# TensorE's first group in 64x64 tiles, other portions for the second group's convolution, and a new order for VectorE's copies of w_in

## The chip, the cores and the metric

The kernel runs on one core of one Trainium2 chip. The time is in device microseconds (us), the median of several runs; lower is better. A profile is one further execution, taken by the hardware profiler; its times count from the start of its span. Engines: PE is TensorE's matmul, PEld its weight load, DVE is VectorE, ACT ScalarE, POOL GpSimd, SP SyncE.

## What is computed

A light convolution over the sequence is followed by a two-layer network:

```python
w = softmax(weight, axis=-1)              # 8 heads x 7 taps
out = np.einsum('hk,bskhg->bshg', w, x_unf)   # x: 8 x 4096 x 192, zeros ahead of each sequence
x = out.reshape(B * S, D)
h = x @ w_in                              # 192 x 2048
g = np.maximum(0.01 * h, h)
return (g @ w_out).astype(np.float32)     # 2048 x 192
```

Every head has 24 of the 192 channels, and one set of 7 taps. Inputs and output are float32; inside, the kernel works in bfloat16 and accumulates in float32.

## The kernel before

**Layout.** The 8 sequences are treated as 4 pairs. A pair's data lies transposed in `xt`: channels in partitions, time along the row. The 192 channels are three chunks of 64 (`CH`); partitions 0 to 63 hold the chunk of the one sequence of the pair (`e` = 0), partitions 64 to 127 that of the other. `yt` holds the convolved data in the same layout. A block is 512 time steps of a pair; there are 32. The first two blocks are cut into halves of 256, called groups 0 to 3 (`groups`, L72); from group 4 on a group is a whole block.

**The stages of a group.** The convolution gives `yt`, by VectorE as seven multiply-adds for each chunk (`conv_jobs`, L209; L222 and L228), or, for parts of groups 0 and 1, by TensorE with diagonal matrices (`pe_conv_jobs`, L244; matmul at L259), whose sums are scaled out of PSUM (L271, L276). `mm1` (L488) multiplies `yt` by `w_in` into a PSUM tile `ph` of two banks (two such tiles are in turn use), and ScalarE's leaky ReLU (L515) makes `g` of it. A group of 256 takes eight steps `u`; each makes two column blocks of 128 hidden units for both sequences. The second layer then multiplies by `w_out`: for groups 0 to 3 in row form (`mm2_one`, L522; its matmul stands at L525), after that as L588 with VectorE's transposes (L610).

**Tiles of TensorE.** A matmul on 64 rows of weights and 64 columns uses a quarter of the array, and four of them may run abreast (64x64); 64x128 gives two abreast, and so does 128x64. In the profile the shape stands with the group, as `64*128`. `mm1` takes weight slices of M columns: M is 128 for groups 0 to 4 and 64 after that (L686). The convolution on TensorE is 64x64. The transposes of x (L167) are 128x64: 128 time steps by 64 channels.

**The first microseconds.** All is laid out by hand, and each engine runs its instructions in the order of the program (`manual_schedule`). Group 0's x is transposed first, then its convolution runs on TensorE (L459 to L474) until about 7.8 us. The loop at L670 then begins with group 0. It has no second-layer work yet. Between its steps of `mm1` the program puts, at fixed places: the transposes of group 1's x (`transpose_first(1)`, L502, inside u = 0), taken out of PSUM by VectorE (`evac_first`, L190, L195); the convolution of group 1, chunk 0 (`pe_0`) and chunk 2 (`pe_2`) on TensorE, in portions after the steps that `CUTS` (L53) names, and chunk 1 (`conv_1`) on VectorE; and after u = 6 the transposes of group 2's x. `pe_0` and `pe_2` have 14 jobs each of two matmuls; `pe_2` writes its halves crosswise (`cross`), so that its two scalings (`evac_2`) handle one half of the partitions each.

**w_in.** It comes in two halves `w_in[0]` and `w_in[1]` of 1024 columns, each by DMAs of rows 0 to 127 into slot 0 and rows 128 to 191 into slot 2. Since both partition halves need all three chunks, copies across the halves follow: `spread_down` (L322) copies slot 0's upper half to slot 1's lower, `spread_up` (L326) copies a lower half to an upper one: slot 0's to slot 1, slot 2's to slot 2. `near` and `far` are columns 0 to 511 and 512 to 1023 of a half. In group 0, steps u = 4 and 5 use the near columns of `w_in[1]`, and u = 6 and 7 the far ones.

**PSUM.** `ph` tiles take two times two banks. The pool `po` has four banks, given out in turn: for transposes, for the convolution's sums and for the second layer's sums. A new tile waits until the one four before it has been read.

**Later.** In group i from 1 on, VectorE convolves group i + 1 (L680). Group 4 is the first of 512. From group 2 on x arrives by DMA (group 2's by the transposes above), and the DMA's own transposes for group 3 (L199) and for blocks 2 and up (L114).

Of the kernel before, what the change touches and what calls it, by code (L numbers as in the profile page):

```python
# [11 lines left out]
BF16 = mybir.dt.bfloat16  # L12
# [3 lines left out]
def kernel(  # L16
# [8 lines left out]
    nc = tc.nc  # L25
# [10 lines left out]
    CH = 64  # L36
    NCH = D // CH
# [3 lines left out]
    HS = SUB // 2  # L41
# [8 lines left out]
    for k in range(K):  # L50
        SKEW += [(2, k), next(pair)]
    SKEW += [(1, 5), (0, 6), (1, 6)]
    CUTS = {1: (0, 6), 3: (6, 11), 5: (11, 14)}  # L53
    GB = 32
    NR = D // (2 * GB)

# [8 lines left out]
    psum_o = ctx.enter_context(tc.tile_pool(name="po", bufs=4, space=bass.MemoryType.PSUM))  # L65
# [56 lines left out]
    def new_xt(rp):  # L122
# [10 lines left out]
    x_rows = {  # L133
        q: const_pool.tile([128, 2, HS, D], BF16, name=f"x_rows{q}") for q in (1, 2)
    }
# [24 lines left out]
    ptr = {}  # L160

    def transpose_first(q, mid=None):
        if q:
            t = psum_o.tile([128, HS, NCH, 128], BF16, name="ptr", tag="po")
            for s, c in product(range(HS), range(NCH)):
                for e in range(2):
                    nc.tensor.transpose(  # L167
                        out=t[e * CH : (e + 1) * CH, s, c, :],
                        in_=x_rows[q][:, e, s, c * CH : (c + 1) * CH],
                        identity=ident,  # L170
                    )
            ptr[q] = [t[:, s] for s in range(HS)]
            return
        ts = [
            psum_o.tile([128, NCH, 128], FP32, name=f"ptr{s}", tag="po") for s in range(HS)
        ]
        for s, t in enumerate(ts):
            if s and mid is not None:
                mid()
            for c in range(NCH):  # L180
                nc.tensor.matmul(
                    out=t[:, c, :],
                    lhsT=x_half[q][:, c, s, :, :].rearrange("p e k -> p (e k)"),
                    rhs=ident,
                    start=True,
                    stop=True,
                )
        ptr[q] = ts

    def evac_first(q, *copies):  # L190
        dst = xt[0][:, :, HALO + q * HT : HALO + (q + 1) * HT]
        dst = dst.rearrange("p c (s k) -> p s c k", s=HS)
        for s, t in enumerate(ptr.pop(q)):
            for cs in (slice(0, 1), slice(1, NCH)) if q == 0 and s else (slice(0, NCH),):
                copies[s](out=dst[:, s, cs], in_=t[:, cs])  # L195

    def transpose_half(q):
# [82 lines left out]
    def run(*lists):  # L280
        for slots in zip_longest(*lists, fillvalue=()):
            for both in slots:
                for job in both:
                    job()
# [14 lines left out]
    for sign, off in ((1, 0), (-1, GRP - 1)):  # L299
        nc.gpsimd.affine_select(  # L300
            out=sel[:, :, 0, :], in_=sel[:, :, 0, :], compare_op=mybir.AluOpType.is_ge,
# [10 lines left out]
    near, far = slice(0, WF // 2), slice(WF // 2, WF)  # L312
# [8 lines left out]
    def spread_down(n, copy=nc.vector.tensor_copy, cols=slice(0, WF)):  # L321
        copy(out=w_in[n][0:CH, 1, cols], in_=w_in[n][CH:128, 0, cols])  # L322

    def spread_up(n, slots=slice(0, 3, 2), cols=slice(0, WF)):
        to = slice(slots.start // 2 + 1, (slots.stop - 1) // 2 + 2)
        nc.vector.tensor_copy(out=w_in[n][CH:128, to, cols], in_=w_in[n][0:CH, slots, cols])  # L326
# [10 lines left out]
    ident = const_pool.tile([128, 128], BF16)  # L337
# [10 lines left out]
    for h in range(2):  # L348
        cs = slice(h * NFC // (2 * RUN), (h + 1) * NFC // (2 * RUN))
        nc.gpsimd.dma_start(  # L350
            out=w_out.rearrange("p (c i) d -> p c i d", i=RUN)[:, cs],
            in_=moe_w_out.rearrange("(c p i) d -> p c i d", p=128, i=RUN)[:, cs],
# [5 lines left out]
    def warm(n, cols=HT, to=wa[:, 0]):  # L358
# [10 lines left out]
        out=nmax, in_=w9[:, 0:K], axis=mybir.AxisListType.X,  # L369
# [3 lines left out]
        out=w9[:, 0:K], in_=w9[:, 0:K], func=mybir.ActivationFunctionType.Exp,  # L373
# [18 lines left out]
    def select(out, parts):  # L392
# [17 lines left out]
        out=taps, in_=wps_hm[..., None].to_broadcast([128, NCH, 2, K + 1, 2])  # L410
# [5 lines left out]
    def diag_wide(c, p):  # L416
# [22 lines left out]
        out=rsum, in0=wml[:, :, K:], scalar=1e-9, in1=taps[:, :, 0, K:, 0],  # L439
# [14 lines left out]
    def act_scale(out, in_, scale):  # L454
# [11 lines left out]
        out=y_of(groups[0], 0), in0=hi[:, :HT], scalar=rsum[:, 0, :], in1=low,  # L466
# [21 lines left out]
    def mm1(grp, u, M):  # L488
        blk, t0, T = grp
        y = yt[blk]  # L490
        nf = ST // T
        ph = psum_h.tile([128, 2, ST], FP32, name="ph", tag="ph")
        chunks = range(NCH)


        wide = not (blk or t0 or u)
        order = [(i, c) for i in range(nf) for c in chunks]
        if wide:
            order = [(i, c) for c in chunks for i in range(nf)]
        for i, c in order:  # L500
            if wide and (i, c) == (0, 2):
                transpose_first(1)  # L502
            f = nf * u + i
            for e in range(2):
                ps = slice(e * CH, (e + 1) * CH)
                for m in range(0, 128, M):
                    nc.tensor.matmul(  # L507
                        out=ph[m : m + M, e, i * T : (i + 1) * T],
                        lhsT=w_in_of(f, e, c, m, m + M),
                        rhs=y[ps, c, t0 : t0 + T],  # L510
                        start=(c == chunks[0] and not (wide and i)),
                        stop=(c == chunks[-1]),
                        skip_group_check=wide,
                    )
        act = nc.scalar.activation(  # L515
            out=g[blk][:, nf * u : nf * (u + 1), :, t0 : t0 + T],
            in_=ph.rearrange("p e (i t) -> p i e t", i=nf),
            func=mybir.ActivationFunctionType.Prelu, alpha=0.01,
        )
        return act  # L520
# [149 lines left out]
    for i, grp in enumerate(groups):  # L670
        blk, t0, T = grp
        steps = T // 64
        if t0 == 0:
            g[blk] = g_pool.tile([128, NFC, 2, ST], BF16, name="g", tag="g")
        quota = plan.get(i, [16] * 4 if T == HT else [5, 5, 6, 5, 5, 6, 8, 8])

        if i == 0:
            ahead = []
        else:
            ahead = conv_jobs(groups[i + 1]) if i + 1 < len(groups) else []  # L680
        per = -(-len(ahead) // steps)
        for j in range(steps):
            early = between.get((i, j), (0, 0))
            for u in range(2 * j, 2 * j + 2):
                mm2_slots(i, early[u % 2])
                mm1(grp, u, 128 if i <= NSW else CH)  # L686
                if i == 0 and u == 0:
                    evac_first(1, nc.vector.tensor_copy, nc.vector.tensor_copy)
                    spread_up(0, slice(2, 3), far)
                    conv_1 = conv_jobs(groups[1], (1,))  # L690
                    run([conv_1[:3]])
                    spread_down(1)
                    spread_up(1, slice(0, 1), near)
                    spread_up(1, slice(2, 3))
                    run([conv_1[3:5]])
                    spread_up(1, slice(0, 1), far)
                    run([conv_1[5:]])
                    pe_0, evac_0 = pe_conv_jobs(groups[1], 0)
                    pe_2, evac_2 = pe_conv_jobs(groups[1], 2, cross=True)
                if i == 0 and u in CUTS:  # L700
                    cut = slice(*CUTS[u])
                    run(pe_0[cut], pe_2[cut])
                if i == 0 and u == 5:
                    evac_0(nc.vector.tensor_scalar_mul)
                    evac_2(nc.vector.tensor_scalar_mul, nc.vector.tensor_scalar_mul)
                if i == 0 and u == 6:
                    transpose_first(2)
                    evac_first(2, nc.vector.tensor_copy, nc.vector.tensor_copy)
            jobs = ahead[per * j : per * (j + 1)]
            if T == ST:  # L710


                jobs = ahead[len(ahead) * j // steps : len(ahead) * (j + 1) // steps]
                for job in jobs:
                    job()
                jobs = []
            mm2_slots(i, quota[j] - sum(early))
            if i == 1 and j == 1:
                load_x(3, transpose_x(2))
            for job in jobs:  # L720
                job()
            if i == 0 and j == 3:
                transpose_half(3)

            last_half = t0 + T == ST
            if i == NSW and j == steps - 1:
                evac_o(LAST - 1)
                slot = NSW * NR * NFC
            if j == steps // 4 and last_half and blk > 0:
                load_x(blk + 3)  # L730
            if j == steps // 2 and last_half and blk > 0:
                transpose_x(blk + 2)
# [35 lines left out]
```

## Time and profile before

| | |
|---|---|
| median of 3 runs | 680.72 us (680.7 to 681.06) |
| span of the profiled execution | 679.2 us |
| TensorE busy in it | 674.9 us, 99% |
| VectorE busy | 481.2 us, 71% |
| ScalarE busy | 517.6 us, 76% |
| granted TensorE clock | 1.000 |
| group 0's steps u begin, end about | 8.09, 17.1 us |
| first L507 of group 1, of group 4 | 17.37, 46.04 us |

The profiled execution is not one of the three timed runs; its time is known by its span, which counts from the first to the last instruction and is 1.5 us below the median. A timeline line gives start, length (both us), engine, line of the program, operation, output <- input, shape and count; `[0.20 <-issue]` says that the engine was idle for 0.20 us before it and what ended that. In it neighbouring instructions of one kind are merged. A line by stretch gives the stretch, its length, then busy time and number of instructions of each engine asked for, the granted clock, the DMA share and GB/s. The program's L numbers are those of the listing above.

### The profile page before, as it was taken

The page shows a single profiled execution, that of the slowest core. Times are in us where ns is not written, and L with a number is a line of the kernel's source. Part 1 is how long each engine was busy: PE and PEld are TensorE (multiplying, and loading weights), DVE is VectorE, ACT ScalarE, POOL GpSimd, SP SyncE. Part 2 cuts the span into 40 slices and gives each one's busy share as a digit, 9 for nine tenths or more (in the row PEclk, how much of TensorE's full clock was granted, in tenths as well). Part 3 has the DMA queues.
Part 4 walks back from the last instruction along what each step waited for, and adds up shares of the span by engine and source line. Part 5 has one row for each costly group of instructions (what it writes and reads, how often), then busy time and mean ns, then how long its engine had stood idle before and what let it go on. Part 6 is the DMA issues. An engine that isn't in the chain of part 4 may idle for free.

```text
span 679.2 us, 27092 instructions
## 1 busy us (share of the span) xinstructions
PE 674.9 (99%) x12442; PEld 446.3 (66%) x12442; DVE 481.2 (71%) x816; ACT 517.6 (76%) x601; POOL 147.4 (22%) x208
## 2 busy tenths in 40 slices
PE   9999999999999999999999999999999999999998
PEld 6997666666666666666666666666666666666667
DVE  7989477866768766778667687667786676876612
ACT  7899877777787777777777777778777777777781
POOL 8455221122211222211222112222022220000000
PEclk9999999999999999999999999999999999999999
DMA  9999755655737656556556566567365573321123
GB/s 149 99 119 104 52 85 83 84 64 67 96 74 93 76 54 86 84 85 86 66 63 92 80 92 78 56 83 94 73 87 69 60 96 71 72 56 33 34 49 94
DMA packets 213970, 53.27 MB, mean 78 GB/s; under 512 B 209312, under 2 KB 213536, under 8 KB 213856
## 3 DMA queue, kind: packets, MB, share of 16 engines
q0 software_dynamic: 98832, 13.97, 30.3%
q1 hardware_dynamic: 115008, 37.57, 28.0%
q8 instruction: 97, 1.59, 0.9%
q14 instruction: 17, 0.14, 0.1%
q10 hardware_dynamic: 16, 0.00, 0.0%
HBM read 28.31 MB, written 25.17 MB: 79 GB/s over the span
## 4 chain that ended last, share of the span: by engine, by line
PE 98%; DVE 1%; ACT 0%; issue 0%; ACTq 0%
PE ph L507 49%; PE acc L588 44%; PE po L525 5%; PE acc L259 0%; DVE diag L420 0%; PE ptr L167 0%; ACT L366 0%; ACTq L288 0%; DVE w_in L322 0%; DVE yt L465 0%; DVE o_sb L638 0%; DVE x_half L155 0%; ACT w L372 0%; DVE w_in L326 0%; ACT junk L366 0%
## 5 line engine op out<-in xcount | busy, mean ns | idle before, releaser
L515 ACT ACTIVATE g<-ph 128x1024 bf16<-128x1024 f32 x512 | 496.6, 1021 | 139.8 <-PE ph L507 139.6
L228 DVE SCALAR_TENSOR_TENSOR yt<-xt,wk,yt 128x512 bf16<-128x512 bf16 (+1 forms) x582 | 380.1, 715 | 0.2
L507 PE MATMUL ph<-yt,w_in 64*64 64x512 bf16 (+2 forms) x6048 | 377.5, 369 | 0.3 <-DVE yt L465 0.3
L588 PE MATMUL acc<-g,w_out 64*64 64x512 bf16 x5568 | 339.9, 376 | 0.0
L507 PEld LDWEIGHTS <-w_in 64*64 64x64 bf16 (+1 forms) x6048 | 229.7, 131 | 103.4 <-issue 1.1
L588 PEld LDWEIGHTS <-w_out 64*64 64x64 bf16 x5568 | 178.2, 118 | 118.8
L96 POOL DMA_DIRECT2D x_bf<-in_x_dram x180 | 133.9, 774 | 407.6 <-DMA xt<-x_bf 405.6
L610 DVE STREAM_TRANSPOSE o_t<-acc 128x512 f32<-128x512 f32 x87 | 72.9, 875 | 182.2 <-PE acc L588 182.2
L525 PE MATMUL po<-w_out,g 64*128 64x192 bf16 (+1 forms) x640 | 36.8, 243 | 0.0
L525 PEld LDWEIGHTS <-g 64*128 64x128 bf16 (+1 forms) x640 | 32.6, 95 | 3.2 <-issue 0.4
L222 DVE TENSOR_SCALAR yt<-xt,wk 128x512 bf16<-128x512 bf16 (+1 forms) x97 | 28.8, 320 | 2.4 <-DMA xt<-x_bf 2.4
L598 ACT COPY junk<-junk 128x1 f32<-128x1 f32 x58 | 11.1, 191 | 4.1
L638 DVE COPY o_sb<-po 128x192 f32<-128x192 f32 x8 | 2.8, 356 | 6.8 <-PE po L525 3.9
L638 ACT COPY o_sb<-po 128x192 f32<-128x192 f32 x16 | 5.1, 323 | 0.3
L259 PE MATMUL acc<-xt,diag 64*64 64x256 bf16 x126 | 4.7, 272 | 0.1
L149 POOL DMA_DIRECT2D x_half<-in_x_dram x6 | 4.3, 732 | 0.9 <-DMA w_in<-in_moe_w_in_dram 0.9
L259 PEld LDWEIGHTS <-diag 64*64 64x64 bf16 x140 | 3.7, 106 | 1.0 <-issue 0.4
L360 PE MATMUL warm<-const-bfloat16-1.0 128*128 128x512 bf16 (+2 forms) x8 | 3.3, 577 | 0.8 <-PEq L752 0.8
L145 POOL DMA_DIRECT2D x_rows<-in_x_dram x4 | 2.9, 746 | 0.0
L316 POOL DMA_DIRECT2D w_in<-in_moe_w_in_dram x5 | 2.9, 593 | 0.0
L360 PEld LDWEIGHTS <-const-bfloat16-1.0 128*128 128x128 bf16 x10 | 1.2, 128 | 2.2 <-issue 2.2
L326 DVE COPY w_in<-w_in 64x512 bf16<-64x512 bf16 (+1 forms) x7 | 2.3, 337 | 0.2
(52 smaller groups left out, 25.9 us busy)
## 6 DMA issues: line engine op xcount, KB each, us to landing
out_dram<-o_t SPq DMA_DIRECT2D x112, 192.0 KB, 4.7
x_bf<-in_x_dram POOLq DMA_DIRECT2D x180, 64.0 KB, 3.1
out_dram<-o_sb SPq DMA_DIRECT2D x8, 192.0 KB, 2.8
xt<-x_bf SPq DMA_TRANSPOSE x90, 3.2
w_out<-in_moe_w_out_dram POOLq DMA_DIRECT2D x2, 384.0 KB, 8.3
out_dram<-o_t SPq DMA_DIRECT2D x8, 96.0 KB, 2.4
out_dram<-o_sb SPq DMA_DIRECT2D x8, 96.0 KB, 1.7
w_in<-in_moe_w_in_dram POOLq DMA_DIRECT2D x2, 256.0 KB, 5.5
```

The source lines that it names most:

```text
L96: ins = nc.gpsimd.dma_start(out=t[:, c, :, e, :], in_=src[2 * rp + e, :, :, c * CH : (c + 1) * CH],)
L222: lambda s=src, d=dst, c=c: nc.vector.tensor_scalar_mul(d, s, wk[:, c, 0:1])
L228: lambda s=src, d=dst, c=c, k=k: nc.vector.scalar_tensor_tensor(out=d, in0=s, scalar=wk[:, c, k : k + 1], in1=d, op0=mybir.AluOpType.mult, ...
L259: lambda k=k, p=p, a=a, ps=ps, to=to, acc=accs[e]: nc.tensor.matmul(out=acc[to, :T], lhsT=diag[c][ps, p, k, :], rhs=xt[0][ps, c, a : a + T ...
L360: nc.tensor.matmul(out=to[:, 0:cols], lhsT=ones[:, 0:128], rhs=ones[:, 0:cols], start=True, stop=True,)
L507: nc.tensor.matmul(out=ph[m : m + M, e, i * T : (i + 1) * T], lhsT=w_in_of(f, e, c, m, m + M), rhs=y[ps, c, t0 : t0 + T], start=(c == chun ...
L515: act = nc.scalar.activation(out=g[blk][:, nf * u : nf * (u + 1), :, t0 : t0 + T], in_=ph.rearrange("p e (i t) -> p i e t", i=nf), func=my ...
L525: return nc.tensor.matmul(out=po[m], lhsT=g[b][ps, fc, e, s * 128 : (s + 1) * 128], rhs=w_out[ps, fc, :], start=start, stop=stop,)
L588: ins = nc.tensor.matmul(out=acc2[gi, r][e * CH : (e + 1) * CH, 0:T], lhsT=w_out_of(ps, fc, r), rhs=g[b][ps, fc, e, t0 : t0 + T], start=fi ...
L598: seal = nc.scalar.copy(out=junk, in_=junk)
L610: nc.vector.transpose(out=osb[gi, 0][:, 0 : T // GB, :, r], in_=acc2.pop((gi, r))[:, 0:T].rearrange("p (j k) -> p j k", k=GB),)
L638: ins = copy(out=o_sb[:, n % 2, :], in_=po.pop(n))
```

## The change

- `mm1` uses slices of 64 columns in group 0 as well (`128 if 0 < i <= NSW else CH`), so that each 64x128 matmul becomes two of 64x64, four abreast.
- The transposes of the x of groups 1 and 2 go in 64x64 tiles: each of 128 time steps by 64 channels becomes two of 64 by 64. The two halves of time (`r`) write to two PSUM tiles `ptr0` and `ptr1` in place of one; `evac_first` copies one tile each, in runs of 64 elements in place of 128.
- The convolution of group 1 on TensorE has its portions after u = 1, 2 and 3 (5, 5 and 4 jobs of each list) in place of u = 1, 3 and 5 (6, 5 and 3). Its sums are scaled after u = 3 in place of u = 5.
- On VectorE four of the seven steps of `conv_1` come before the copies of `w_in[1]`, in place of three. The copies are six of 512 columns, the near ones first, in place of four (two of 1024 columns). The other three steps of `conv_1` come between and behind the scalings.

```diff
-    CUTS = {1: (0, 6), 3: (6, 11), 5: (11, 14)}
+    CUTS = {1: (0, 5), 2: (5, 10), 3: (10, 14)}
...
         if q:
-            t = psum_o.tile([128, HS, NCH, 128], BF16, name="ptr", tag="po")
+            ts = [
+                psum_o.tile([128, HS, NCH, CH], BF16, name=f"ptr{r}", tag="po")
+                for r in range(2)
+            ]
             for s, c in product(range(HS), range(NCH)):
-                for e in range(2):
+                for r, e in product(range(2), range(2)):
+                    ps = slice(r * CH, (r + 1) * CH)
                     nc.tensor.transpose(
-                        out=t[e * CH : (e + 1) * CH, s, c, :],
-                        in_=x_rows[q][:, e, s, c * CH : (c + 1) * CH],
-                        identity=ident,
+                        out=ts[r][e * CH : (e + 1) * CH, s, c, :],
+                        in_=x_rows[q][ps, e, s, c * CH : (c + 1) * CH],
+                        identity=ident[ps, ps],
                     )
-            ptr[q] = [t[:, s] for s in range(HS)]
+            ptr[q] = ts
             return
...
+        if q:
+            dst = dst.rearrange("p c (s r k) -> p r s c k", s=HS, r=2)
+            for r, t in enumerate(ptr.pop(q)):
+                copies[r](out=dst[:, r], in_=t)
+            return
...
-                mm1(grp, u, 128 if i <= NSW else CH)
+                mm1(grp, u, 128 if 0 < i <= NSW else CH)
                 if i == 0 and u == 0:
                     evac_first(1, nc.vector.tensor_copy, nc.vector.tensor_copy)
                     spread_up(0, slice(2, 3), far)
                     conv_1 = conv_jobs(groups[1], (1,))
-                    run([conv_1[:3]])
-                    spread_down(1)
+                    run([conv_1[:4]])
                     spread_up(1, slice(0, 1), near)
-                    spread_up(1, slice(2, 3))
-                    run([conv_1[3:5]])
+                    spread_down(1, cols=near)
+                    spread_up(1, slice(2, 3), near)
+                    spread_down(1, cols=far)
                     spread_up(1, slice(0, 1), far)
-                    run([conv_1[5:]])
+                    spread_up(1, slice(2, 3), far)
...
-                if i == 0 and u == 5:
+                if i == 0 and u == 3:
                     evac_0(nc.vector.tensor_scalar_mul)
-                    evac_2(nc.vector.tensor_scalar_mul, nc.vector.tensor_scalar_mul)
+
+                    def after(n):
+                        def scale(*args):
+                            run([conv_1[n : n + 1]])
+                            nc.vector.tensor_scalar_mul(*args)
+
+                        return scale
+
+                    evac_2(after(4), after(5))
+                    run([conv_1[6:]])
```

## The prediction

> **What bounds the kernel now.** I read the page first, then busy time by stretch, then the timelines of the weight loads, VectorE and ScalarE over the changed microseconds, and last the hand-over at 46 us.
>
> ```profile
> PE 674.9 (99%) x12442; PEld 446.3 (66%) x12442; DVE 481.2 (71%) x816; ACT 517.6 (76%) x601; POOL 147.4 (22%) x208
> PE 98%; DVE 1%; ACT 0%; issue 0%; ACTq 0%
> ```
>
> TensorE is busy all the way and is nearly the whole chain of waits, so time can only be gained by starting its long steady part earlier. A busy PE may still be draining. The stretches (PE, PEld, DVE, ACT, POOL busy):
>
> ```profile
> 8.09:17.29 9.20, 9.20 (x181) 7.21 (x181) 8.09 (x21) 8.01 (x10) 7.03 (x12) 1.00 1.24 162
> 17.29:46.04 28.75, 28.75 (x608) 28.56 (x606) 28.71 (x65) 26.37 (x34) 17.30 (x23) 1.00 1.19 109
> ```
>
> The changed code runs in the first. In the second VectorE is as full as TensorE: it convolves groups 2, 3 and 4 without a pause, and that matters below. The weight loads (PEld) show what the mixed tiles cost:
>
> ```profile
> 10.11 0.58 PEld L259 LDWEIGHTS <-diag 64*64 64x64 bf16 x24 [0.20 <-DVE xt L195]
> 10.89 1.24 PEld L507 LDWEIGHTS <-w_in 64*128 64x128 bf16 x24 [0.20 <-issue]
> 12.33 0.47 PEld L259 LDWEIGHTS <-diag 64*64 64x64 bf16 x20 [0.20 <-issue]
> 13.00 0.25 PEld L507 LDWEIGHTS <-w_in 64*128 64x128 bf16 x5 [0.20 <-issue]
> 13.46 1.02 PEld L507 LDWEIGHTS <-w_in 64*128 64x128 bf16 x19 [0.21 <-DVE w_in L326]
> ```
>
> Each change of shape has 0.20 us of idle in front. In the convolution before 8 us, four 64x64 matmuls of 256 columns start every 0.109 us (6.28, 6.39, 6.50 ...), so the 24 from 10.11 should last 0.656; the next shape starts 0.78 later. A change therefore costs 0.125 net. The row at 13.46 is a real wait: the second half of w_in was not yet copied across the partition halves.
>
> **TensorE, part by part.** (a) Between 8.09 and 17.02 there are ten changes of shape (into and out of transposes twice, convolution three times). All go; one comes in before L525, which keeps 64x128. Nine times 0.125 is 1.13 us. (b) Group 0's 96 matmuls of 64x128 become 192 of 64x64. A pair of the old takes 0.109, a quad of the new 0.109 by the convolution rows: nothing gained or lost. (c) Each set of 12 transposes becomes 24. Pitch goes with columns in the trace: 0.216 for 512 (46.04 on), 0.109 for 256, 0.055 for the present 128. For 64 columns no row exists. Low end 0.028 a quad (0.17 a set), high end today's 0.055 (0.33, no gain, if the weight load sets the pace); I take 0.17, on the line of the three rows: 0.16 saved twice. (d) The convolution is 56 matmuls in either cut. So at most 1.13 + 0.32 = 1.45 us of TensorE work goes, and less survives, as the walk shows.
>
> A rule speaks against (c). The trace starts the four matmuls of a quad within 0.01 us of each other. The Trainium skill ("TensorE: Matmul & The Clock Gate", Back-to-back issue gap) gives 1 to 64 columns a floor of about 25 ns from start to start; no row here has so few columns. By it a set would take 24 x 25 = 600 ns, u7 below would end 0.35 later, and the forecast would be 680.5 in place of 680.4.
>
> **The walk.** A quad is 0.109, a step u of group 0 six quads, 0.656. The start, 8.09, stays: it follows VectorE's yt (L465). First two chunks to 8.53, transposes to 8.70, then a wait: yt's third chunk leaves VectorE at 8.39 + 0.49 = 8.88, so 8.93 (with 0.05 for the release, as at 46.21 below) to 9.15. u1 to 9.81. The convolution needs xt from VectorE (9.22 + 0.62 = 9.84, unchanged, as those copies stand behind a w_in copy that ends at 9.20): 9.89 to 10.44. u2 11.09, convolution 11.64, u3 12.30, convolution 12.73. u4 needs three w_in copies, which VectorE ends at about 12.50, 12.81 and 13.11 (below): its third quad starts at 13.17, u4 ends at 13.60, u5 at 14.26. From here ScalarE limits: an activation of g takes 1.02 and they follow at 0.92 to 1.02, longer than a bare u, with two ph buffers. By these rows it starts 0.31 after a step's last quad:
>
> ```profile
> 14.13 2.98 ACT L515 ACTIVATE g<-ph 128x1024 bf16<-128x1024 f32 x3 [0.41 <-PE ph L507]
> 17.33 2.99 ACT L515 ACTIVATE g<-ph 128x1024 bf16<-128x1024 f32 x3 [0.22 <-PE ph L507]
> ```
>
> u4's activation runs 13.80 to 14.82, u5's 14.72 to 15.74. So u6 runs 14.87 to 15.53, transposes to 15.70, u7 15.79 to 16.45. One change of shape and three pairs of L525 (0.25) bring group 1's first matmul to 16.83, where it is at 17.37 now. w_out's first half is no obstacle: POOL's wait for it ends at 16.02. The new bank order puts L525's second bank behind the last scaling of group 1's third chunk, about 16.50 on VectorE, before 16.58. TensorE alone would be 0.54 earlier.
>
> **VectorE.** Its rows now:
>
> ```profile
> 10.59 1.00 DVE L228 SCALAR_TENSOR_TENSOR yt<-xt,wk,yt 128x256 bf16<-128x256 bf16 x2
> 12.21 0.42 DVE L322 COPY w_in<-w_in 64x1024 bf16<-64x1024 bf16 x1 [0.61 <-DMA w_in<-in_moe_w_in_dram]
> 12.64 0.77 DVE L326 COPY w_in<-w_in 64x512 bf16<-64x512 bf16 x2
> 13.45 1.00 DVE L228 SCALAR_TENSOR_TENSOR yt<-xt,wk,yt 128x256 bf16<-128x256 bf16 x2
> 14.48 0.29 DVE L326 COPY w_in<-w_in 64x512 bf16<-64x512 bf16 x1
> 14.80 1.00 DVE L228 SCALAR_TENSOR_TENSOR yt<-xt,wk,yt 128x256 bf16<-128x256 bf16 x2
> 15.72 0.48 DVE L271 TENSOR_SCALAR yt<-acc,rsum 128x256 bf16<-128x256 f32 x1
> 16.23 1.00 DVE L276 TENSOR_SCALAR yt<-acc,rsum 64x256 bf16<-64x256 f32 x2
> 17.27 0.62 DVE L195 COPY xt<-ptr 128x384 bf16<-128x384 bf16 x2
> ```
>
> From 12.21 to 17.27 are 5.06 us: copies 1.56, four conv steps 1.95, three scalings 1.55. One conv step (0.52) moves into the 0.61 of idle before 12.21, where the w_in DMA hides it; 0.06 of idle is left. Four copies become six of 512 columns. At the 0.29 of the rows at 8.07, 8.91 and 14.48, plus gaps of 0.01 to 0.03, they make 1.80. The upper end is 0.55, what a downward copy of 512 took at 6.97: six at that are 3.4. I take 0.29, since in this same stretch the downward copy took 0.42 for twice the columns. The sum is 1.80 + 1.46 + 1.55 = 4.81, **0.25 earlier**. The regrouped copies of the transposes stay at 0.31 each, same elements; their shorter runs could make them 0.05 dearer, which is nothing beside the ends above.
>
> Group 1's second chunk now ends VectorE's list, at 17.0, 0.1 later than TensorE wants it; the lead there shrinks to 0.44. What then decides stands 29 us later:
>
> ```profile
> 17.26:46.16 28.90, 28.86 (x65) 1.00 1.19 109
> 45.42 0.73 DVE L228 SCALAR_TENSOR_TENSOR yt<-xt,wk,yt 128x512 bf16<-128x512 bf16 x1
> 46.21 0.11 PEld L507 LDWEIGHTS <-w_in 64*128 64x128 bf16 x1
> ```
>
> The first row is VectorE alone, 28.86 busy of 28.90: all it does up to 46.16 hangs on when it began, at 17.27. Its last conv step of group 4 ends at 46.15, and at 46.21 a weight load follows that TensorE needs for 46.26. The slack there is 0.05. So a lead on TensorE is cut to VectorE's 0.25 plus 0.05: **0.30 us** remain, and nothing later waits that nearly: VectorE idles again from 46.16.
>
> **Sum.** The profiled span is 679.2; the median of the runs shown is 680.72, about 1.5 above, which I take as what lies around the span and as unchanged. 679.2 - 0.30 = 678.9, and so **680.4**.
>
> **Rivals.** (1) TensorE's whole lead arrives, because VectorE's copies overlap (as 12.64 and 12.85 do, by 0.08) and its list ends 0.45 earlier: 680.1 to 680.2. For it: several conv steps and scalings would also overlap. Against it: today's rows have mostly gaps. (2) Slower: w_in's last part comes late, at VectorE's third copy. It is issued at 6.13 and lands 6.6 later, 12.73; the copy wants it at 12.81. TensorE's instructions are loaded by DMA too (page, queue q8): one load between 9 and 11 us, the next between 16 and 18, each some 0.96 us of one engine (3.0% of 16 engines over 2 us). With 1.6 times the instructions the second load comes near 12 us. If it stands before w_in's last rows, VectorE's third copy starts 0.9 late: -0.30 becomes +0.6, 681.3. It turns slower than before from a delay of 0.3 us on. The same case holds copies at 0.55: the two downward ones add 0.5 (680.9), all six 1.6 (682.0). Against it: the load may use another engine. (3) A load of instructions stalls TensorE itself in 8 to 16 us, where it now eats 8 instructions per 0.109 us, twice the steady rate. No PE row shows such a wait today; the convolution before 8 us ran at that rate for 84 matmuls. One or two loads of 0.96, less the 0.24 by which TensorE's lead exceeds what arrives: 681.2 to 682.1. (4) The change doesn't do what it says: four small tiles with w_in's strided weights don't run abreast. At half speed that is 5.2 us more, 685. Against it: L507 runs 24 such matmuls of 512 columns in 1.30 us throughout the steady part.
>
> **How the numbers follow.** Forecast 0.55; (1) 0.17; (2) 0.19; (3) 0.06; (4) 0.01; a gain past (1), by an order of things later on that I don't see, 0.02. The range takes the forecast, (1) and (2) with its bounds: 679.8 to 681.9. About 0.2%, 1.36 us, is what a measurement of this kernel can tell from no change. The likeliest cases lie within it: over 0.2% faster, 0.03 (more than all that (a) and (c) remove); over 0.2% slower, 0.06 ((4), the far ends of (2) and (3)); within, 0.91.
>
> **What would show it.** Right: no 0.20 idle between 8.7 and 16 us, one before L525; group 0 in quads 0.109 apart; VectorE without idle before 12.15; its copies of the transposes near 17.0; group 1's matmuls near 16.9; the end of VectorE's convolution near 45.9 with TensorE's wait just after it. Wrong: w_in copies of 0.5, an idle before the third, PE rows waiting on issue inside a shape, or a shift on TensorE at 46 us that is not VectorE's.

## The result, and the profile after

The changed kernel takes 683.82 us (median of 5 runs, 683.38 to 685.21) against 681.06 for the kernel before in the same runs: 1.0045 times as long, 95% interval 1.0034 to 1.0056. The forecast was 680.4, the range 679.8 to 681.9; the changed kernel is slower by 2.8 us and lies outside. The profiled execution spans 681.9 us, 2.7 more than before.

Most lines shift by nine: `mm1`'s matmul is now L516, the convolution L268, the second layer's row form L534; the transposes move from L167 to L171. The page's chain of waits and the groups of costliest instructions that answer to the first lines shown of before:

```profile
PE 674.6 (99%) x12562; PEld 447.9 (66%) x12562; DVE 482.1 (71%) x818; ACT 517.7 (76%) x601; POOL 147.7 (22%) x208
...
PE 98%; DVE 1%; issue 1%; ACT 0%; ACTq 0%
...
L516 PE MATMUL ph<-yt,w_in 64*64 64x512 bf16 (+3 forms) x6144 | 379.0, 368 | 2.4 <-issue 1.8
...
L268 PE MATMUL acc<-xt,diag 64*64 64x256 bf16 x126 | 4.7, 271 | 1.1 <-issue 1.0
```

The same two groups before, in which hardly any idle time stood:

```profile
L507 PE MATMUL ph<-yt,w_in 64*64 64x512 bf16 (+2 forms) x6048 | 377.5, 369 | 0.3 <-DVE yt L465 0.3
...
L259 PE MATMUL acc<-xt,diag 64*64 64x256 bf16 x126 | 4.7, 272 | 0.1
```

TensorE's busy time is 0.3 us less, yet the span grew. The new share in the chain is "issue": time in which TensorE waited for nothing that the profile shows, 1.8 us within `mm1` and 1.0 us within the convolution. The timeline of the weight loads shows where (idle time before a row in brackets):

```profile
8.09 0.41 PEld L516 LDWEIGHTS <-w_in 64*64 64x64 bf16 x15 [0.59 <-issue]
...
10.38 0.78 PEld L516 LDWEIGHTS <-w_in 64*64 64x64 bf16 x24
...
12.43 0.47 PEld L268 LDWEIGHTS <-diag 64*64 64x64 bf16 x19 [1.25 <-issue]
12.87 0.72 PEld L516 LDWEIGHTS <-w_in 64*64 64x64 bf16 x24
...
14.95 0.67 PEld L516 LDWEIGHTS <-w_in 64*64 64x64 bf16 x24 [0.20 <-issue]
16.05 0.56 PEld L516 LDWEIGHTS <-w_in 64*64 64x64 bf16 x20 [0.42 <-issue]
18.63 0.14 PEld L516 LDWEIGHTS <-w_in 64*64 64x64 bf16 x3 [2.02 <-issue]
```

The idle 0.20 at each change of shape is gone, as it should be. In its place stand two stops, and neither is at a place where the program waits: the first comes one weight load into a portion of the convolution, the second after 20 of the 24 matmuls of step u = 6. By stretches of TensorE (stretch, length, busy time and number of matmuls, granted clock, DMA share, GB/s):

```profile
8.09:11.41 3.32, 3.29 (x116) 1.00 1.03 146
11.41:12.43 1.02, 0.00 (x0) 1.00 1.35 169
12.43:16.82 4.39, 4.14 (x128) 1.00 1.32 188
16.82:18.63 1.81, 0.00 (x2) 1.00 1.31 85
```

Ahead of the first stop TensorE works as forecast, with 116 matmuls in 3.3 us. The stops take 1.02 + 1.81 = 2.83 us. Group 1's first matmul is at 20.08 (17.37 before, +2.71), group 4's at 48.75 (46.04, +2.71), the end at 681.9 (+2.7): what is lost before 19 us is never won back. Between the two stops lie 128 matmuls with 128 weight loads, 256 instructions.

### The profile page after: what moved, and what is told of

Read it like the earlier page. It is cut to its first block, busy times and chain, and to the rows that moved or that the text cites. A ratio compares the mean times of both kernels' runs of the same rounds, so it can differ in the third digit from the quotient of the medians.

```text
span 681.9 us, 27334 instructions
## 1 busy us (share of the span) xinstructions
PE 674.6 (99%) x12562; PEld 447.9 (66%) x12562; DVE 482.1 (71%) x818; ACT 517.7 (76%) x601; POOL 147.7 (22%) x208
## 4 chain that ended last, share of the span: by engine, by line
PE 98%; DVE 1%; issue 1%; ACT 0%; ACTq 0%
PE ph L516 49%; PE acc L597 44%; PE po L534 5%; DVE diag L429 0%; PE acc L268 0%; ACT g L524 0%; ACT L375 0%; ACTq L297 0%; DVE w_in L331 0%; DVE yt L474 0%; PE ptr L171 0%; DVE o_sb L647 0%; DVE x_half L155 0%; ACT w L381 0%; DVE w_in L335 0%
## 5 line engine op out<-in xcount | busy, mean ns | idle before, releaser
L516 PE MATMUL ph<-yt,w_in 64*64 64x512 bf16 (+3 forms) x6144 | 379.0, 368 | 2.4 <-issue 1.8
L516 PEld LDWEIGHTS <-w_in 64*64 64x64 bf16 (+1 forms) x6144 | 231.9, 131 | 104.9 <-issue 3.2
L534 PE MATMUL po<-w_out,g 64*128 64x192 bf16 (+1 forms) x640 | 37.8, 243 | 0.0
L534 PEld LDWEIGHTS <-g 64*128 64x128 bf16 (+1 forms) x640 | 34.0, 95 | 2.4 <-issue 0.4
L607 ACT COPY junk<-junk 128x1 f32<-128x1 f32 x58 | 11.1, 191 | 4.1
L268 PE MATMUL acc<-xt,diag 64*64 64x256 bf16 x126 | 4.7, 271 | 1.1 <-issue 1.0
L268 PEld LDWEIGHTS <-diag 64*64 64x64 bf16 x140 | 4.0, 106 | 1.8 <-issue 1.3
```

Source lines behind the costliest of these rows:

```text
L268: lambda k=k, p=p, a=a, ps=ps, to=to, acc=accs[e]: nc.tensor.matmul(out=acc[to, :T], lhsT=diag[c][ps, p, k, :], rhs=xt[0][ps, c, a : a + T ...
L516: nc.tensor.matmul(out=ph[m : m + M, e, i * T : (i + 1) * T], lhsT=w_in_of(f, e, c, m, m + M), rhs=y[ps, c, t0 : t0 + T], start=(c == chun ...
L534: return nc.tensor.matmul(out=po[m], lhsT=g[b][ps, fc, e, s * 128 : (s + 1) * 128], rhs=w_out[ps, fc, :], start=start, stop=stop,)
L607: seal = nc.scalar.copy(out=junk, in_=junk)
```

## The theory and its rival

**Theory A.** TensorE's instructions are loaded by DMA (queue q8) in blocks of 256. Two blocks fit; the next one is asked for when a block is used up, and TensorE stops when it reaches a block that is not there. In the first 20 us the load queues behind data. The change puts 240 more instructions before 20 us and so reaches the blocks' limits too early.

**Theory B.** The stops are waits among the engines that the new order makes: VectorE's copies and scalings, or the PSUM banks, which the transposes now take in pairs.

In the trace before, the q8 loads begin at 9.94, 16.50, 20.57, 26.71 and 32.96 us. From the third on, each begins 0.2 to 0.6 us after the moment when TensorE passes another 256 recorded instructions (702 at 20.38, 958 at 26.41, 1214 at 32.36). Counted back, the first two were asked for at about 7.1 and 13.8, and were 2.8 and 2.7 us late. The request is not in the trace; its time is this count.

## The experiments

**mm1 alone.** One edit to the kernel before:

```diff
-                mm1(grp, u, 128 if i <= NSW else CH)
+                mm1(grp, u, 128 if 0 < i <= NSW else CH)
```

> The kernel before with one part of the change: group 0's mm1 in 64x64 tiles, 192 more instructions on TensorE before 17 us. Theory A (instruction loading): TensorE's instructions come by DMA in blocks of 256; the load of a block starts only when the block two before it is used up, waits 3 to 5 us behind data in the first 20 us, and TensorE stops when it reaches a block that has not come. Then TensorE stops with 'issue' near 11.3 us until about 12.4 and again near 16.5 until about 18.6, and the median is 682.5 to 683.9. Theory B (a wait among the engines made by the new order: VectorE's copies and scalings, or the PSUM banks given to the transposes in pairs): no stop longer than 0.5 us here, 680.0 to 681.0.

Measured: 684.85 us against 681.08, ratio 1.0054 (1.0042 to 1.0067), above the range expected. The clock has a share in that: three of the six executions, the profiled one among them, have a mean granted clock of 0.998 and took 685.58 to 686.20 us; the other three, at 1.000, took 683.45 to 684.13. (What the clock did comes last below.) The stops are there, without the new order and without banks in pairs, and now in other places of the program, the second in the middle of the transposes:

```profile
13.24 0.41 PEld L507 LDWEIGHTS <-w_in 64*64 64x64 bf16 x15 [1.13 <-issue]
...
19.17 0.14 PEld L167 LDWEIGHTS <-x_rows 128*64 128x64 bf16 x3 [1.83 <-issue]
```

What the places have in common is the count. These are the stretches up to each stop's end, first of the changed kernel, then of this one (stretch, length, then busy time and count of PE, PEld, DVE, ACT, POOL):

```profile
0.00:12.42 12.42, 10.12 (x222) 7.04 (x223) 9.12 (x35) 8.96 (x17) 11.52 (x26) 1.00 0.90 136
12.42:18.62 6.20, 4.14 (x128) 3.56 (x128) 4.31 (x12) 3.02 (x4) 3.94 (x6) 1.00 1.32 158
```

```profile
0.00:13.23 13.23, 11.31 (x222) 7.94 (x223) 9.51 (x36) 9.07 (x17) 11.38 (x25) 1.00 0.87 133
13.23:19.16 5.93, 4.21 (x128) 3.60 (x128) 3.93 (x9) 3.98 (x4) 4.63 (x7) 1.00 1.36 155
```

In both, TensorE stops after 222 matmuls and 223 weight loads, and again after 128 more of each, whatever the instruction is. Theory B has no reason for that.

**The transposes alone**: `transpose_first` and `evac_first` of the change put into the kernel before.

```diff
-            t = psum_o.tile([128, HS, NCH, 128], BF16, name="ptr", tag="po")
+            ts = [
+                psum_o.tile([128, HS, NCH, CH], BF16, name=f"ptr{r}", tag="po")
+                for r in range(2)
+            ]
...
```

> The kernel before with only the transposes of groups 1 and 2 in 64x64 tiles (48 more instructions on TensorE, two PSUM banks a set). Theory A: the block limits are reached about 0.6 and 1.0 us earlier than before (13.1 and 19.3 us), still after the loads are there (12.4 and 18.6): no stop, 680.6 to 681.3. Theory B, if the banks in pairs are the cause: a stop of 0.5 us or more in 9 to 19 us, 681.5 or above.

Measured: 681.08 against 681.08, ratio 1.0001 (0.9992 to 1.0009), no stop. The banks in pairs are not the cause.

**The order alone**: the new `CUTS`, the portions and VectorE's new order, all tiles as before.

```diff
-    CUTS = {1: (0, 6), 3: (6, 11), 5: (11, 14)}
+    CUTS = {1: (0, 5), 2: (5, 10), 3: (10, 14)}
...
-                    run([conv_1[:3]])
-                    spread_down(1)
+                    run([conv_1[:4]])
...
```

> The kernel before with only the new portions of the convolution and the new order on VectorE (no instruction more on TensorE). Theory A: no stop; by the forecast's sum for VectorE 0 to 0.3 us earlier, 680.7 to 681.1 against 681.0. Theory B, if the order is the cause: TensorE stops for 1 us or more between 11 and 19 us, 682 or above.

Measured: 681.66 against 681.08, ratio 1.0008 (1.0000 to 1.0017), above the 680.7 to 681.1 expected. No stop of the kind, but no gain either: at the edge of what can be told, it is slower.

**All but mm1**: the change with `128 if i <= NSW else CH` put back.

> The change with group 0's mm1 left in 64x128 tiles (48 more instructions than before, in place of 240). Theory A: no stop over 0.5 us that ends with an instruction block, 680.6 to 681.7. If the transposes or the order together make the stops: 683 or above.

Measured: 681.50 against 680.75, ratio 1.0011 (1.0002 to 1.0020), no stop of the kind. So both stops hang on `mm1`'s 192 instructions; the 0.75 us that are lost without them are something else. The 48 instructions of the transposes already come to the edge: in this run and the one with the transposes alone the first block's load ended at 11.51 and 11.55 us, and the first instruction behind the limit began 1.38 and 1.39 us later, as soon after the load as at the end of the stops (1.3 to 1.46).

The profile of this run also shows why the order gains nothing, in the weight loads, in the only wait of `mm1`'s matmuls for ScalarE (us in total, times, longest) and in ScalarE's activation of u = 4:

```profile
15.38 0.59 PEld L516 LDWEIGHTS <-w_in 64*128 64x128 bf16 x11 [0.62 <-DVE yt L237]
```

```profile
PE ph L516 <- ACT g L524: 0.5, 1, 0.5
```

```profile
14.31 1.02 ACT L524 ACTIVATE g<-ph 128x1024 bf16<-128x1024 f32 x1 [0.32 <-PE ph L516]
```

Step u = 6 starts 0.05 us after that activation ends (14.31 + 1.02 = 15.33): it waits for the `ph` buffer, as the row of the matmuls says, and VectorE is named for the weight loads by a release that lies near. In the kernel before, a portion of the convolution stood after u = 5 and filled ScalarE's time; now they are all spent by u = 3. Group 1's first matmul comes at 17.41 here, 17.37 before. This execution was the fastest of the eleven (680.91), and its span, 679.2, is that of the kernel before: it shows that there is no gain, and not where the median loses 0.75, which stays open.

**Tiny matmuls**, the direct test of a count: the kernel before with 64 extra matmuls that compute nothing anyone reads.

```diff
+    for n in range(64):
+        r, e = divmod(n % 4, 2)
+        ps = slice(r * CH, (r + 1) * CH)
+        nc.tensor.matmul(
+            out=(wps, wa)[r][e * CH : (e + 1) * CH, 1, 500:504],
+            lhsT=ones[ps, 0:CH], rhs=ones[ps, 0:4], start=True, stop=True,
+        )
     spread_up(0, slice(0, 1), far)
```

> The kernel before with 64 extra matmuls of 4 columns in 64x64 tiles (128 more instructions), put where TensorE idles 0.4 us ahead of group 0; they write to unused columns of PSUM and nothing of the change is in it. They take some 0.5 us of TensorE, of which 0.4 is idle time. Theory A (blocks of 256 instructions come late): the block limit that was crossed at 13.7 us is now reached at about 10.5, the block is there at about 12.4, so TensorE stops for 1.5 to 2 us, and the median is 682.2 to 683.0. If only the new tiles or the new order make the stops: 680.9 to 681.4.

Measured: 683.15 against 680.75, ratio 1.0036 (1.0024 to 1.0049), but this decides nothing: `wps` was still being read by ScalarE, and the tiny matmuls waited 1.1 us for that. TensorE then came to the limit late and stopped there for less than 0.4 us. The repeat writes to `wa` alone (`out=wa[e * CH : (e + 1) * CH, r, 500:504]`):

> The run with 64 tiny matmuls again, their results now in a PSUM tile that no engine still reads, so that they don't wait for ScalarE as they did (1.1 us, which spoiled that run). The kernel before otherwise. Theory A: the block limit is reached at about 10.5 to 10.8 us, the block is usable 1.4 us after its load ends (11.0 to 11.2), so TensorE stops for 1.4 to 2 us within the convolution or the steps there, and the median is 682.0 to 682.8 (before: 680.8). Without such a limit the added matmuls cost at most 0.5 us: 680.8 to 681.4.

Measured: 683.66 against 681.23, ratio 1.0033 (1.0021 to 1.0045), more than expected. The stretch up to the stop's end, and the two stretches of TensorE that hold the stop and what follows:

```profile
0.00:13.85 13.85, 9.87 (x222) 6.88 (x222) 9.62 (x36) 8.08 (x16) 11.39 (x25) 1.00 0.87 135
```

```profile
11.00:13.90 2.90, 0.34 (x16) 1.00 1.21 178
13.90:17.30 3.40, 3.40 (x36) 0.50 1.47 188
```

The old tiles, the old order, the old banks, and TensorE stops at the same count (444 in the records, 445 in the others), for 2.83 us, in the convolution: its block's load began only at 11.48 us here. That settles A against B. The last row is a second price: the granted clock was 0.50 for 3.4 us after the stop. It was paid in this execution, the slowest of the six (685.47, mean clock 0.997); the other five, at 1.000, took 682.92 to 684.03.

**Do the loads wait behind data?** First only the data of later groups were put off, from 10 us to behind group 0's step 5 (`load_first(3)` and `load_x(2)` with a dependency on its activation), in the changed kernel:

```diff
-    load_first(3)
-    load_x(2)
...
-                mm1(grp, u, 128 if 0 < i <= NSW else CH)
+                act = mm1(grp, u, 128 if 0 < i <= NSW else CH)
+                if i == 0 and u == 5:
+                    load_first(3, act)
+                    load_x(2)
```

> The changed kernel, with group 3's x and block 2's x loaded only after group 0's step 5 (some 0.6 MB less data in the DMA queues between 10 and 15 us). Theory A: the first stop (11.4 to 12.4 us) stays at about 1 us, since nothing before 10 us is moved; the second block's load starts at 13 to 15 us in place of 16.2, and the second stop of 1.8 us shrinks to below 0.6: 681.6 to 682.8. If instruction loads do not wait behind data, or the stops are not instruction loading: both stops stay, 683.4 to 684.2.

Measured: 684.32 against 681.08, ratio 1.0054 (1.0041 to 1.0067). The expectation failed: the second block's load began at 15.97 and the second stop stayed at 1.74. Most of this data is issued after the second request (11.1 us), behind it in any case; what lies ahead is `w_out`, issued at 8.1 to 9.5. So next `w_out`'s second half was put behind step 1:

```diff
+                if i == 0 and u == 1:
+                    load_w_out(1, act)
+                    load_first(3)
+                    load_x(2)
```

> The changed kernel with w_out's second half, and POOL's loads behind it, issued only after group 0's step 1 (at about 11.5 in place of 8.8 us). Theory A, sharpened by the last runs: an instruction block waits behind the data issued before it was asked for (at 11.1 us for the second), whatever is issued after. Then the second block's load starts at about 14 in place of 16.2, the stop at 16.6 shrinks from 1.8 to below 0.6, the first stop stays at 1.0 to 1.3: 681.8 to 683.0. If the wait is not for data ahead of it: 683.4 to 684.4.

Measured: 683.36 against 680.75, ratio 1.0037 (1.0025 to 1.0050). Half right: the median lies above the range, the second load came at 15.82 and not at 14, the second stop shrank to 1.19 and not to 0.6; `w_out`'s first half was still ahead. Then the loads ahead of the first request were put off too, w_in's last part, group 2's x and `w_out`'s first half until VectorE's first step on yt (L465 of the kernel before) ends, at about 8.1 us:

```diff
+    load_w_in(1, 128, after=ins)
+    load_first(2)
+    load_w_out(0)
```

> As the last one, and besides w_in's last part, group 2's x and w_out's first half are issued only after 8.1 us (6.1 to 8.8 before), behind the request for the first block at 7.05 us. Theory A: the first block's load starts at 9 to 9.6 in place of 10.15, the first stop shrinks from 1.0 to 0.2 to 0.7, the second stays below 0.6: 681.0 to 682.4, unless the later w_in delays VectorE. If the wait is not for data ahead of it: 683.4 to 684.4.

Measured: 682.26 against 680.75, ratio 1.0028 (1.0018 to 1.0039); stops of 0.65 and 0.92. The time is in the range, the second stop above the 0.6 expected, and of the 0.60 by which the first is shorter, 0.27 is only TensorE's later arrival (11.40 in place of 11.14). At last nearly everything was put behind the requests:

```diff
-    spread_down(0, cols=near)
+    load_w_in(1, 0, after=spread_down(0, cols=near))
+    load_w_in(1, 128)
+    load_first(2)
...
+                if i == 0 and u == 1:
+                    load_w_out(0, act)
+                    load_w_out(1)
+                    load_first(3)
+                    load_x(2)
```

> The changed kernel with w_in's second half and group 2's x issued only after 7.5 us (5.6 before), and w_out and what follows only after group 0's step 1 (about 11.4), so that both requests for instruction blocks (7.05 and 11.1 us) find little data ahead. Theory A: block loads start at 7.5 to 9 and at 11.5 to 13.5 us, both stops fall below 0.4 us, and the forecast on record without its rival 3 is tested: 680.3 to 681.5, unless w_out comes too late for L534 (then a wait for DMA, not for issue). If block loads do not depend on data ahead: stops as in the changed kernel, 683.4 or above.

Measured: 681.51 against 681.23, ratio 1.0005 (0.9996 to 1.0013), at the upper end of the range expected. The changed tiles and order are all there, and both stops are gone:

```profile
15.09 0.63 PEld L517 LDWEIGHTS <-w_in 64*64 64x64 bf16 x23 [0.63 <-issue]
...
17.46 0.20 PEld L535 LDWEIGHTS <-g 64*128 64x128 bf16 x6 [0.82 <-DMA w_out<-in_moe_w_out_dram]
```

What remains is the wait for ScalarE's buffer (15.09, at a step's start) and a new one for `w_out`, now late. In order of the data left ahead of the requests:

| kernel | 1st block's load begins, idle of PEld | 2nd block's load begins, idle of PEld |
|---|---|---|
| changed | 10.15, 1.25 | 16.21, 2.02 |
| group 3 and block 2 later | 10.04, 1.27 | 15.97, 1.74 |
| w_out's second half later | 10.38, 1.54 | 15.82, 1.19 |
| also w_in's last part, group 2's x, w_out | 9.79, 0.65 | 14.94, 0.92 |
| all later | 7.88, none | 13.11, none |

The view of the DMA queues for the stretch from 11.2 to 16.2 us of the changed kernel, and for 13.1 to 14.1 of the one with all loads later (packets, MB, the packets' time as a share of 16 engines):

```profile
q0 software_dynamic: 1282, 0.93, 126.4%
```

```profile
q0 software_dynamic: 51, 0.07, 59.9%
q8 instruction: 1, 0.02, 6.0%
```

In the first, the 5 us after the second request, the data queue moved 1282 packets and no instruction block came.

Two controls. The kernel before with the same later loads:

> The kernel before with the same later loads, to see what they cost by themselves. Theory A: TensorE had no stop there, so nothing is gained: 680.6 to 681.4, a little more if w_in or w_out come late. A gain of over 0.5 us would mean that data or instructions had held the kernel before up, too.

Measured: 681.29 against 681.23, ratio 1.0002 (0.9993 to 1.0011): the order of the loads by itself is worth nothing. And `w_out`'s first half moved one step ahead of the run with all loads later, to cure its wait:

```diff
-                if i == 0 and u == 1:
+                if i == 0 and u == 0:
                     load_w_out(0, act)
-                    load_w_out(1)
+                if i == 0 and u == 1:
+                    load_w_out(1, act)
```

> As the run with all loads later, but w_out's first half goes out after group 0's step 0 (about 10.4 us) in place of step 1, since L534's kind of matmul waited 0.8 us for it there. Theory A: the second block is asked for at 11.1 and now has up to one w_out half ahead of it, but 1.5 us were to spare, so no stop over 0.4 us returns; the wait for w_out goes, TensorE's group 1 begins near 17.0 and the median is 680.5 to 681.3, beside 681.2 for the kernel before: a tie or a gain of up to 0.1%. If the block comes too late after all: a stop between 15 and 18 us, 681.5 to 682.5.

Measured: 681.97 against 680.87, ratio 1.0012 (1.0003 to 1.0021). No stop for a block came back, but the expectation failed: the wait for `w_out` stayed (0.89) and the median lies above the range. The half went out at 11.2 us and not at 10.4, half a microsecond ahead of the run with all loads later (11.7), and took 6.7 us to land in place of 5.7. No version beat the kernel before.

## Why the prediction was wrong, step by step

**What bounds the kernel**: right. TensorE stayed busy all the way and the loss before 19 us stood in full at the end.

**(a) Changes of shape**: right, none costs 0.20 in group 0 any more; the 0.20 at 14.95 stands between two rows of `mm1`. **(b) Quads**: right; 24 matmuls of L516 have 0.65 in the chain at 13.17, as forecast. **(c) Transposes**: right in kind. In the run with the transposes alone a set of 24 weight loads shows as

```profile
8.65 0.27 PEld L171 LDWEIGHTS <-x_rows 64*64 64x64 bf16 x24 [0.19 <-issue]
```

and 0.31 passes from this row's start to the next shape's (8.96), the change of shape of about 0.125 included: 0.18 to 0.19 for the set, where 0.17 was taken. The rule of the Trainium skill that was weighed there ("TensorE: Matmul & The Clock Gate", Back-to-back issue gap), 25 ns from start to start, would make 0.60. The measurement decides: four tiles abreast start closer together than that. The prediction was mistaken that no row has so few columns. The kernel before has three matmuls of 48 columns on the whole array:

```profile
4.20 0.24 PE L396 MATMUL warm<-w9p,sel 128*128 128x48 bf16 x3
```

They start 28 and 25 ns apart (4.204, 4.232, 4.257), as the rule says. In the set of transposes above it is the quads that start some 31 ns apart, and the four of a quad within 0.01 us: there the 25 ns bind a tile and not the array.

**The walk** held until it met the first block limit: the one weight load of the next portion that still came stands at 11.07, where the walk has 11.09, and `mm1` goes on at its pitch behind each stop. In the run with all loads later TensorE came to L535 at about 16.64 (17.46 less the 0.82 of waiting), where the walk has 16.58.

**VectorE**: right in size. The six copies take from 12.14 to 14.02, 1.88 where 1.80 was taken, and the steps between the scalings interleave as drawn:

```profile
12.14 0.29 DVE L335 COPY w_in<-w_in 64x512 bf16<-64x512 bf16 x1
12.46 0.29 DVE L331 COPY w_in<-w_in 64x512 bf16<-64x512 bf16 x1
...
13.45 0.58 DVE L335 COPY w_in<-w_in 64x512 bf16<-64x512 bf16 x2
14.30 0.48 DVE L280 TENSOR_SCALAR yt<-acc,rsum 128x256 bf16<-128x256 f32 x1 [0.27 <-PE acc L268]
...
16.75 0.48 DVE L237 SCALAR_TENSOR_TENSOR yt<-xt,wk,yt 128x256 bf16<-128x256 bf16 x1
19.21 0.36 DVE L199 COPY xt<-ptr 128x384 bf16<-128x384 bf16 x1 [1.98 <-PE ptr L171]
```

Its list ends at 17.23 in spite of 0.27 of waiting for the first stop; without that it is the forecast's 17.0. Then it stands idle for 1.98, because TensorE's transposes are behind the second stop. So the lead that the forecast gave to VectorE was there and was lost in one place.

**The sum's base** was 0.2 low. It took the time as 1.5 us above the span; in the executions that have both on record the time is 1.66 to 1.83 above it (once 2.02), so a span of 679.2 stands for some 680.9. This is small beside the 2.8 lost.

**The step that failed is the loading of TensorE's instructions.** The walk takes every instruction to be there when TensorE comes to it, and the sum has no term for it; rival (3), a load of instructions that stalls TensorE, was given 0.06 and a price of one or two load times of 0.96 (681.2 to 682.1). The runs showed two stops of 1.02 and 1.81 us instead. The rival's mechanism was right; three things were wrong in the reckoning. The price left out the wait ahead of the load (3.0 and 5.1 us from the count to its start) and the time behind it: TensorE goes on 1.3 to 1.46 us after the load's packet ends (11.13 to 12.43, 17.17 to 18.63). The evidence against it, 84 matmuls of the convolution at full rate, was no evidence: those came out of blocks that were there from the start, since no load stands in the trace before 9.94. And rival (2) reckoned with a second load near 12 us and looked for its harm at w_in; w_in's last part landed at 11.9, and the harm was to TensorE itself. What would have told it, had the count been known: the first load began at 9.94 in the kernel before, and with its 0.97 and the 1.3 to 1.46 us behind it no instruction past the first 446 could be had before 12.2, while the walk wanted it at 11.1.

**The gain of 0.30** remains unseen. With the stops gone the changed tiles tie with the kernel before (1.0005, 0.9996 to 1.0013), with 0.82 us of waiting for `w_out` in it. Whether 0.3 us would appear if that wait could be avoided too was not shown. One pair of profiles speaks for the forecast's limit at 46 us, and for less than it left: with the transposes alone TensorE came to group 1 0.31 us earlier (17.06) and VectorE began its list 0.41 earlier (16.86), but that list ended only 0.13 earlier (46.02) and group 4 began 0.12 earlier (45.93); the medians of the two are the same. The new order is no gain as long as `mm1` keeps its old tiles, without the new transposes or with them (1.0008 and 1.0011).

## What to carry to other kernels

More and smaller instructions can cost more than their engine time: where an engine runs through its instructions at twice the usual rate while the DMA queues are full of first loads, count the instructions against the blocks (here 256) and look when their loads start and what data was issued ahead of them. A stop that the profile puts down to "issue", in the middle of a series of equal instructions and at the same count in different kernels, was such a load here. It goes away with fewer instructions (the runs without `mm1`'s small tiles), or by issuing data that is not needed yet after the moment a block is asked for; the latter took both stops away here, and gave the time back only as far as the data then came in time.

## What the runs showed of the hardware

- TensorE's instructions come in blocks of 256 (16 KB, the page's queue q8; 0.9 to 1.5 us each for the first two blocks, up to 2.0 later). A load started 0.0 to 0.6 us after the count that asks for it in the quiet part of the kernel before (third to seventh block), 2.7 to 6.5 us after it for the first two blocks with data ahead, and 0.4 to 2.1 in the three runs with nearly all the data held back.
- From the end of a load's packet to the first instruction out of it passed 1.3 to 1.46 us in every stop.
- The clock may fall after a stop. With `mm1` alone the second stop is followed by half clock for 3.4 us, as in the run with tiny matmuls above:

```profile
17.20:19.20 2.00, 0.28 (x10) 1.00 1.29 83
19.20:22.70 3.50, 3.50 (x48) 0.51 1.65 100
```

In the profiled execution of the changed kernel it did not (clock 1.00 throughout, with a stop of 1.81). The Trainium skill ("TensorE: Matmul & The Clock Gate", "What's actually happening") has half rate after an idle window of about 3.4 us; here stops of 1.9 and 2.8 us were enough in two executions. The traces' records of the clock suggest why some stops cost it and others do not: the half clock lasted 3.41 us in both (from 19.27 and 13.88), and full clock had been granted 13.65 and 10.24 us earlier, four and three times 3.41. Counted in such steps from the first grant, a whole stop lay in the step ahead of the half clock in these two. In the changed kernel (first grant at 3.80) a step ends at 17.45, in the middle of the second stop, and no step has more than 1.4 us without a new instruction; with `w_out`'s second half later a stop of 1.59 lay in one step and the clock stayed. No run varied this alone.
- Full clock was first granted between 3.6 and 6.3 us after the start, at a different time in each profiled execution. With the order alone, where it came at 6.15, quads of the convolution start 0.21 to 0.22 us apart up to 6.08 and 0.11 apart from 6.23 on. Of the eight executions whose loads are alike up to there, the seven that had it by 5.6 us began group 0 at 8.09 to 8.10, and this one at 8.33. This may be part of the scatter of the timed runs, for which there is no trace.
